# Two transformer layers on one core: a table of priority offsets for the list scheduler, and accumulators zeroed by products

## The chip, the cores and the metric

The kernel runs on one core of a Trainium2 chip. The core has five engines that run side by side, each with its own instruction stream: TensorE (PE, matrix products, with its weight loads shown apart as PEld), VectorE (DVE), ScalarE (ACT), GpSimd (POOL) and SyncE (SP, which here only issues DMA transfers). They wait for each other with semaphores. PE writes its products into PSUM, which has eight banks of 512 fp32 columns on 128 partitions; DVE and ACT read them from there. The metric is the time of one execution on the device, in microseconds (us); less is better.

## The reference

The input has 2048 tokens of width 512. Attention has 32 heads of width 16 and a causal window of 256 tokens; the feed-forward part has width 1792. The same weights are used twice.

```
x = A_x
x = x + _A_ref(_layernorm(x), A_wqkv, A_wo)          # sliding window attention
x = x + _B_ref(_layernorm(x), B_w1, B_b1, B_w2, B_b2)  # gelu(x @ w1 + b1) @ w2 + b2
x = x + _A_ref(_layernorm(x), A_wqkv, A_wo)
x = x + _B_ref(_layernorm(x), B_w1, B_b1, B_w2, B_b2)
return x
```

Inside `_A_ref`, scores are `q k^T / 4`, masked to `0 <= i - j < 256`, followed by a softmax, a product with `v`, and a product with `wo`.

## The kernel before

**Tiling.** X stays in SBUF as 16 tiles of 128 tokens (two layers make 32 tile visits). Attention works in blocks of 256 tokens: 8 in each layer, 16 in all. The feed-forward part works in ten jobs of two or four tiles.

**One attention block.** `lnq` and `kv` normalise the two tiles (statistics on DVE in `L547` and `L549`, the inverse root on POOL in `L551` and `L554`, the normalised tile xn on DVE in `L557`), transpose them on PE, and form Q, K and V. K is written with every second head masked to zero (`L625`). `visit` forms the scores: ten visits for each block, 64 small products each, into four banks; ACT takes the exponential from PSUM into E (`L699`). `mask` multiplies E by the causal mask on DVE (`L711`) or POOL (`L714`). `pv` multiplies E with V, to which a column of ones is appended, so that the sum of each softmax row comes out as one more row. Its result is copied from PSUM into OD on DVE (`L766`) or ACT (`L768`).

**Normalising.** For each half block, seven DMAs on SP do it: Dc gathers the sums from OD (`L769`), DVE takes the reciprocal (`L772`), scr_r writes it to DRAM (`L774`), Rn reads it back spread over the partitions (`L776`), and four copies move the odd heads inside OD (`L779`). Then OT = OD x Rn on DVE or POOL (`L784`), and `outproj` multiplies OT with Wo on PE. The residual is added on DVE (`L590`), the tile is normalised again, and POOL adds the second bias (`L819`).

**Feed-forward.** `mlp` multiplies with W1; the gelu runs on ACT directly from PSUM (`L858`), or after a copy with bias by DVE (`L846`) from SBUF (`L849`). Then it multiplies with W2 and adds the residual; in the last layer each finished tile is stored (`L870`).

**Order.** All this is given to a planner, `_Plan`, as nodes: engine, planned duration in ns, what is read and written, a priority `prio` (smaller goes first), an allocation of PSUM banks, and for some nodes alternatives `alt` on another engine with a handicap. `_Plan.run` is a list scheduler: it walks through planned time, and for each free engine it takes the ready node with the smallest priority. A handicap is added to the priority for the alternative engine (`ACT_H = 300` for copies on ACT, `POOL_H = 60` for masks on POOL), so it also decides which engine takes the node. What comes out is one fixed order for each engine, the engine of each movable node and the banks; `_Sched` then puts in the semaphore waits. On the chip each engine follows its order whatever the real durations are. Priorities run by block: block b starts at `200.0 * b`; inside it, a visit g stands at `16 * g`, the two halves of `pv` stand 80 apart, and the projections of the next block stand at 110 (Q) and 140 (K, V).

**Start.** Two DVE memsets (`L503`) set all eight PSUM banks to zero, and everything on PE waits for them. SP issues the loads in the order of their priorities: X tiles 0 to 1, 2 to 3, the three parts of Wqkv (`L516`), X 4 to 7, Wo, X 8 to 15, W1 (`L523`), W2 (`L524`), b2b (`L527`), b1raw (`L526`). In the profile all products that a helper issues have the line `L32`, and all transposes `L36`.

## Time and profile before

| | us |
|---|---|
| median of 3 runs (551.79 to 552.99) | 552.06 |
| the profiled execution | 548.19 |
| its span, first to last instruction | 546.5 |
| mean granted clock of PE | 0.956 of full speed |

The costliest groups of instructions, with the number of them, their busy time and the mean of one:

| engine, what | count | busy us | mean ns |
|---|---|---|---|
| ACT exponential, E from PSUM (`L699`) | 330 | 305.8 | 1009 |
| POOL masks (`L714`) | 96 | 112.5 | 1182 |
| DVE masks (`L711`) | 160 | 75.2 | 493 |
| ACT gelu from PSUM (`L858`) | 92 | 51.1 | 584 |
| ACT copies of OD (`L768`) | 21 | 21.5 | 1022 |
| DVE copies of OD (`L766`) | 11 | 13.4 | 1218 |
| DVE zeroing of PSUM (`L503`) | 2 | 3.5 | 1765 |

Busy times of different engines overlap, and a busy PE is modelled from the size of its products. "Granted clock" is the share of PE's full clock that the chip let through. The chain of waits follows the work back from the last instruction to what released each step; an engine's time that is not on it was hidden behind other work. Times in a list of the timeline are counted from the start of the span.

### The profile page before, as it was taken

The numbers are of one execution on the slowest core, as the hardware profiler recorded it, in microseconds if no ns is written. First come the engines' busy times: TensorE is split into PE (matmuls) and PEld (weight loads), VectorE is DVE, ScalarE is ACT, GpSimd is POOL, SyncE is SP. The second block draws the span as 40 slices with busy tenths as digits, with TensorE's granted clock in tenths as the row PEclk, the third lists the DMA queues.
The fourth block names the chain that finished last, engine by engine and source line by source line (L and its number), as shares of the span: only waits on it lengthen the run. The fifth ranks groups of instructions, "written<-read, shape, count | busy, mean of one in ns | idle before, by whom it ended". The sixth has DMA issues, their size and how long they took to land.

```text
span 546.5 us, 19716 instructions
## 1 busy us (share of the span) xinstructions
PE 458.2 (84%) x8849; PEld 246.2 (45%) x8945; DVE 358.9 (66%) x684; ACT 437.7 (80%) x521; POOL 222.5 (41%) x306
## 2 busy tenths in 40 slices
PE   3878697889579998899978879997898788969997
PEld 2545255455344443445444444443444343434644
DVE  6889675578586766886596768864576565764241
ACT  2798678788887898899899889898769987797633
POOL 6576523544264232652275225571144431422030
PEclk9979799999799999999999999997999989979999
DMA  8801101011111101110111101100121101111110
GB/s 276 312 13 52 38 12 36 22 35 31 35 33 34 35 4 39 32 37 25 34 34 34 33 10 39 52 14 22 34 61 45 33 3 48 59 34 38 35 49 20
DMA packets 26401, 25.01 MB, mean 46 GB/s; under 512 B 11596, under 2 KB 19660, under 8 KB 26316
## 3 DMA queue, kind: packets, MB, share of 16 engines
q1 hardware_dynamic: 26316, 23.74, 14.6%
q8 instruction: 70, 1.15, 0.9%
q14 instruction: 15, 0.12, 0.1%
HBM read 16.39 MB, written 2.62 MB: 35 GB/s over the span
## 4 chain that ended last, share of the span: by engine, by line
PE 44%; DVE 19%; DMA 18%; ACT 8%; SPq 5%; issue 4%; POOL 0%; DVEq 0%
PE ps L32 43%; DMA Rn<-scr_r 12%; ACT E L699 5%; SPq L779 4%; DMA scr_r<-Rc 4%; DVE OT L784 3%; DVE KT L625 3%; DVE E L711 3%; DVE stat L547 2%; DMA Dc<-OD 2%; DVE X L590 2%; ACT OD L768 2%; PE ps L36 1%; DVE QT L534 1%; DVE gT L846 1%
## 5 line engine op out<-in xcount | busy, mean ns | idle before, releaser
L699 ACT ACTIVATE E<-ps 128x1024 bf16<-128x1024 f32 (+1 forms) x330 | 305.8, 1009 | 26.5 <-PE ps L32 24.4
L714 POOL TENSOR_TENSOR E<-E,mask 128x512 bf16<-128x512 bf16 x96 | 112.5, 1182 | 153.5 <-ACT E L699 153.4
L32 PE MATMUL ps<-xnTB,W_sb 128*128 128x512 bf16 (+1 forms) x531 | 107.8, 340 | 6.3 <-issue 1.9
L32 PE MATMUL ps<-W_sb,gT 128*128 128x512 bf16 x407 | 102.1, 380 | 5.1 <-issue 2.1
L711 DVE TENSOR_TENSOR E<-E,mask 128x512 bf16<-128x512 bf16 x160 | 75.2, 493 | 35.4 <-ACT E L699 35.0
L32 PE MATMUL ps<-QT,KT 32*64 32x320 bf16 (+4 forms) x3072 | 71.2, 268 | 18.2 <-ACT E L699 14.2
L32 PE MATMUL ps<-xnTA,Wqkv_sb 128*128 128x256 bf16 x512 | 72.6, 284 | 8.2 <-DVE KT L625 4.6
L590 DVE TENSOR_TENSOR X<-X,ps 128x512 bf16<-128x512 bf16 x64 | 43.5, 683 | 48.0 <-PE ps L32 47.8
L32 PEld LDWEIGHTS ps<-xnTB,W_sb 128*128 128x128 bf16 x560 | 50.5, 99 | 48.3 <-issue 6.8
L858 ACT ACTIVATE gT<-ps,b1T 128x512 bf16<-128x512 f32 (+1 forms) x92 | 51.1, 584 | 17.5 <-PE ps L32 17.2
L32 PEld LDWEIGHTS ps<-W_sb,gT 128*128 128x128 bf16 x448 | 40.0, 98 | 49.0 <-issue 5.4
L32 PE MATMUL ps<-E,Va 64*17 64x128 bf16 (+3 forms) x3840 | 52.1, 240 | 11.5 <-DVE E L711 3.2
L32 PEld LDWEIGHTS ps<-QT,KT 32*64 32x64 bf16 x3072 | 28.7, 105 | 70.3 <-ACT E L699 48.2
L32 PEld LDWEIGHTS ps<-xnTA,Wqkv_sb 128*128 128x128 bf16 x512 | 46.1, 101 | 27.8 <-DVE KT L625 6.1
L551 POOL TENSOR_SCALAR veps<-statmv 128x1 f32<-128x1 f32 x64 | 16.0, 258 | 93.7 <-DVE statmv L549 93.2
L32 PEld LDWEIGHTS ps<-E,Va 64*17 64x17 bf16 x3840 | 41.0, 88 | 27.4 <-PE ps L32 8.4
L768 ACT ACTIVATE OD<-ps 128x1024 f32<-128x1024 f32 x21 | 21.5, 1022 | 28.8 <-PE ps L32 28.6
L846 DVE TENSOR_SCALAR gT<-ps,b1T 128x512 bf16<-128x512 f32 (+1 forms) x48 | 32.6, 681 | 17.3 <-PE ps L32 16.4
L547 DVE BATCH_NORM_STATS2 stat<-X 128x6 f32<-128x512 bf16 x64 | 43.1, 683 | 0.9
L784 DVE TENSOR_TENSOR OT<-OD,Rn 128x256 bf16<-128x256 f32 x46 | 23.7, 546 | 30.2 <-DMA Rn<-scr_r 29.9
L36 PE MATMUL ps<-ident,xn 128*128 128x128 bf16 x256 | 25.7, 232 | 21.0 <-DVE xn L557 9.9
L625 DVE TENSOR_TENSOR KT<-ps,parmask 128x1024 bf16<-128x1024 f32 x32 | 38.8, 1217 | 6.6 <-PE ps L32 6.5
(44 smaller groups left out, 394.7 us busy)
## 6 DMA issues: line engine op xcount, KB each, us to landing
Rn<-scr_r SPq DMA_DIRECT2D x32, 256.0 KB
OD<-OD SPq DMA_DIRECT2D x128, 32.0 KB
W_sb<-in_B_w_dram SPq DMA_DIRECT2D x2, 1792.0 KB
out_dram<-X SPq DMA_DIRECT2D x16, 128.0 KB
Wqkv_sb<-in_A_wqkv_dram SPq DMA_DIRECT2D x3, 512.0 KB
X<-in_A_x_dram SPq DMA_DIRECT2D x1, 1024.0 KB
X<-in_A_x_dram SPq DMA_DIRECT2D x2, 256.0 KB
X<-in_A_x_dram SPq DMA_DIRECT2D x1, 512.0 KB
```

The costliest lines, as they stand in the source:

```text
L32: return self.e.matmul(*a, **k)
L36: return self.e.transpose(*a, **k)
L547: add("dve", lambda e, B: e.bn_stats(stat6[:, k6, :], X[:, t, :]), 590, reads=["X%d" % t], writes=["st%d" % k6], prio=prio)
L590: add("dve", lambda e, B: e.tensor_tensor(out=X[:, t, :], in0=X[:, t, :], in1=ps[:, B[g][0], :], op=ALU.add), d_psum(512), reads=["X%d" % ...
L625: add("dve", lambda e, B, g=g, i=i: e.tensor_tensor(out=KT[:, kb, :, 2 * i : 2 * i + 2, :].rearrange("p a c q -> p a (c q)"), in0=ps[:, B[ ...
L699: a = (add("act", lambda e, B, g_=g_, gi=gi, o=o, e1=e1, n=n: e.activation(E[:, 2 * gi : 2 * gi + 2, e1 : e1 + n], ps[:, B[g_][0] : B[g_][ ...
L711: add("dve", lambda e, B: e.tensor_tensor(out=Ew, in0=Ew, in1=Mw, op=ALU.mult), 340.0, lock=True, reads=["E%d%s" % (es, x) for es in ess f ...
L714: alt=(("pool", lambda e, B: e.tensor_tensor(out=Ew, in0=Ew, in1=Mw, op=ALU.mult), POOL_M * n, POOL_H),))
L768: alt=(("act", lambda e, B: e.activation(OD[:, s, :, :], ob(B), AF.Copy, scale=1.0), d_act(1024), ACT_H),))
L784: mul = lambda e, B, c=c, o=o: e.tensor_tensor(out=OT[:, bs, c, :], in0=OD[:, s, 0, o : o + 256], in1=Rn[:, rs, o : o + 256], op=ALU.mult)
L846: add("dve", lambda e, B, g=g, fc=fc: e.tensor_scalar(out=gT[:, fc, 0:M], in0=ps[:, B[g][0], 0:M], scalar1=b1T[:, fc : fc + 1], scalar2=No ...
L858: gelu_last[0] = add("act", lambda e, B, g=g, fc=fc: e.activation(gT[:, fc, 0:M], ps[:, B[g][0], 0:M], AF.Gelu_apprx_tanh, bias=b1T[:, fc ...
```

## The change

`_Plan` gets two strings, `tune`. Every different triple of engine, rounded priority and duration gets a number in the order in which it first occurs; the character at that number in the first string, minus 80 (the letter P is zero), is added to the node's priority, and the one in the second string, times four, is added to the handicaps of its alternatives. The characters span -46 to +46. The first string has 1597 characters, 1382 of them not P; the second has 1576, 339 of them not P.

The two DVE memsets of PSUM become one memset of a new SBUF tile `zero` (128x512) and eight products of it with itself, one for each bank; that node is added twice (`NZ = 2`).

The planned duration of the Dc transfer goes from 1900 to 1980 ns, that of Rn from 3000 to 3600 ns.

```diff
-    def __init__(self, pools):
+    def __init__(self, pools, tune=("", "")):
+        self.keys = {}
+        self.tune = tune
...
         i = len(self.nodes)
+        k = self.keys.setdefault((eng, round(prio, 3), dur), len(self.keys))
+        step, lean = (float(ord(t[k]) - 80) if k < len(t) else 0.0 for t in self.tune)
+        prio += step
+        alt = tuple((e2, f2, d2, h2 + 4.0 * lean) for e2, f2, d2, h2 in alt)
...
-            alts=((eng, fn, dur, 0.0),) + tuple(alt), done=False,
+            alts=((eng, fn, dur, 0.0),) + alt, key=k, done=False,
...
+    NZ = 2
...
+        zero = sb("zero", [P, D])
...
+        TUNE = ((
+            '&J"Od*TQ)4I5KHPatpSx_#@QBTlr]Q~2IE5b"~STUK]UAS{6p[cVbHmkZEPYPeB"p)Zp_PP~_~"\\KPDEM0K[]QQB~LGP%K)7PNqP'
...
+        ), (
+            'PPPPPPPPPPPPPPPPPPPPPPPPPPPPQPMPPPPPPPPPP"PUPPPPPP*PPPPPPPPrPPiiPP~PPXAPP>7PPPP~PPPPP,PPJ8PP]PP)PPPC'
...
-        })
+        }, TUNE)
...
-        for h in range(2):
-            add("dve", lambda e, B, h=h: e.memset(ps[:, 4 * h : 4 * h + 4, :], 0.0), 1680, writes=["ps:init%d" % h], prio=-200)
+        add("dve", lambda e, B: e.memset(zero[:], 0.0), 120, writes=["zero"], prio=-300)
+
+        def clear(e, B):
+            for b in range(8):
+                r = e.matmul(ps[:, b, :], zero[:, 0:P], zero[:], start=True, stop=True)
+            return r
+
+        for h in range(NZ):
+            add("pe", clear, 8 * mm(512), reads=["zero"], writes=["ps:init0", "ps:init1"], prio=-200, geo="f")
...
-                    ["Dc%d" % rs], reads=ods, prio=pr - 50, dur=1900.0, issue=660.0)
+                    ["Dc%d" % rs], reads=ods, prio=pr - 50, dur=1980.0, issue=660.0)
...
-                    ["Rn%d" % rs], reads=["SR%d" % rs], prio=pr - 50, dur=3000.0, issue=710.0)
+                    ["Rn%d" % rs], reads=["SR%d" % rs], prio=pr - 50, dur=3600.0, issue=710.0)
```

In the first string the ninth character onward belongs to the loads: `)4I5KHPatpSx`, for X 0 to 1, X 2 to 3, the queries, keys and values of Wqkv, X 4 to 7, Wo, X 8 to 15, W1, W2, b1raw and b2b.

More of the change, by code (lines that the diff above doesn't have):

```diff
@@ L462, in bass_interleave_layers__sliding_block__dense_activation_gelu__prompt_kernel @@
         psb = ps[:].bitcast(dt.bfloat16)
+        TUNE = ((
+            '&J"Od*TQ)4I5KHPatpSx_#@QBTlr]Q~2IE5b"~STUK]UAS{6p[cVbHmkZEPYPeB"p)Zp_PP~_~"\\KPDEM0K[]QQB~LGP%K)7PNqP'
+            'SYa8ZVg9&-o"xVPP?bdDD;l/^ACPp]QPU;M+hSXU<ST+GPrs-PP\\\\@0^PP;xPh=SLXi;"VHP`nM9/zBpHIKbWauVL@"?NMW\\Ps=Q'
+            'mTUCC~"YX?GoopNO[eUw`MeO^ERPPDobLTF"PFYj"IULPL.P",&qW"J3qr"t~PUKP[O\'U}PECP~,[PJ.\'K.UQePBZQv\\:pXl"?j~'
+            'X{.abZ^tSbFQ~~5Xf\\@%PP^\\pPPS)8`b`.IP]Ncq3a7JtPlEv-]PQP$QPK&PPT`PPOkHPAWYV]@TL^S"Pmb*P6,*viVOPPJA"RuP'
+            '(ZEukBLP"J|qPdP"P.PROQNDO-:~2f&FGkB2P"fPd(P\'kN@DU<HPJBB-PPN}~=F"PrPNHY:G"I~R1lPesI6TRR6%J1VWPP]3Oh4G'
+            'PG<~],g@}Q3j"PGTdR[\\Lj"RDF8e^oPH]SR"N.VIixPAP\\MPI.|PPB"PT^H`O"S<Pa&OP{P|$ecPT&jP-pPMTSDuuPSP\\@PUzPx_'
+            'AATa\'iLH7w@6W~RY~o&PSbXL#~NPy%X|z~APyPPL`#UgABNJbNm?TOPh"9d[>O&K4WYiPJpPG_aM:0kSRdy7PgevHP^P\'?o,~60O'
+            '@:PZQTQtP"`PX8jhPlLE^<wPI=LYIPBX}GRPUyEPP.=hZe-^l8kSJT~PP0F\\S)EP-1RPvNRh*gV~>O~fPireN8_OBXMK3P@4WSjY'
+            'E7"K8PC~HMT(+QPBPSPJE"P-,@\'KE2M~Th-XE=VXPQl\\YP^P8XPPPnLY+OPI*P]#PT]LXfQcX"Z%\\\\Z\\8=^g?^PX6XRMIWPPT=s}'
+            'PcZ>P9y9encgw~XweXg4yJP~HJ~JK`ZSPm@@:_NE,,YO;M?PR]PR@KjxASi,~#"~K}+(PP_Q4jXTPKSP"PXP"_|"PgP8T$+-TF]j'
+            'pwH*]LUFOQaLP~LP"k>,GM((P~PP.~2\'TW$IPV+HPX>FR@LaPSz\\][`~~[TmKfO*PqI%4{P3SCT[|Y~G5rHc`H~Wa\\N`F&a^>n\\P'
+            "ePP)_qBYIGFxpP6~Y0jNanSNVPPET/J@@PGPP[RXI#a6W?M=Yp<c8:4{'VKR?PYBAt@~:wmJ@fYf%@KdPW|~]P~PYP`PIM~=YY??"
+            'ckTD"K"m~EPPWa)h"bW>U(~EJU~2$aQ<~>IM2XN?T8Pr)a/~AKP`P@~PWPx~PXPPJ^[H2OP~9U~-Q~bMLF|u___ysvYLDDqinXq~'
+            'hiT@F+rWSMNH"JpP"+ZQ)BN]u%ryPQxn"TOPPb"PO7inbQ.P"+SPgIPO(YeV.HXQEMWK(0>XURy41P:^H]&M;r:_u?~PU*\\PaPNS'
+            'IEMU\\~P+5kDP&0Ce:VZM"Pdi7DSkYPP,;qPiSf?V""gGJT/O~vAPH|$YP""+lIJYFT8T_JVt~a"+Z"NLd8\\AaXW*ZP:xz~"OOOFC'
+            '\'LPjuiOJMN&P;u@O/PEPPcC2{J_kCm[VP~"n,:^SSP",OP}[/DPMVqODp&@~?Ic]N"QXM>HXPC~w?IPPPq"9<PW`GuGMB&P-Q'
+        ), (
+            'PPPPPPPPPPPPPPPPPPPPPPPPPPPPQPMPPPPPPPPPP"PUPPPPPP*PPPPPPPPrPPiiPP~PPXAPP>7PPPP~PPPPP,PPJ8PP]PP)PPPC'
+            'mPmPPPPP,PPPPPPPP(PPPPPPPPPKPPPPPPPSPaPPPsPPePPnRPPPPPMCPP"}PP~PsPPPPPGPPCPPP3PPFLPP#~PPPPPPP"PPPPPP'
+            'PPrPPPPPPPPP?PPPPPPP9PsPPPPPP?PP>PPPhPPT8PPq"PPPP"PPPPPTPPZ|PPPPPPPPPPPPPPPPPPPPPPP~PP~rPP-TPDPPPPPO'
+            'PPPPPPPP"PPPPPPPPPBPPPPPPPhPVPPPlPPVPPi~PP[PPT"PPfJPPGPWPPPPP@PP@SPPPPPPPPPPPPPPPPPPPPPPP1PP6CPPxBPZ'
+            'PPPPPePPPPPPPP~PPPPPPPPPzPPPPPPPIPOPPPPPPPPP=KPPMPPP,PP8XPP[PPPPPPP~PP"~PPNPP_:PPn~P=PPPPP"PPPPPPPP6'
+            'PPPPPPPPPnPPPPPPP\'PPPPP~PPAPPj"PPPPP~^PPSaPP_PHPPPPPPPPZ[PPPPPPPPPPPPPPPPPPPPPPPPPPPPPP0,PPyQPEPPPPP'
+            '"PPPPPPPP"PPPPPPPPPePPPPPPPSP1PPP2PP~PP:PPPmPPBUPPzOPP_PkPPPPP-PP~\\PP"PPP"PP)mPwPPPPPPPPPPPPPPFPPPPP'
+            'PPPP~PPPPPPP"PDPPP@PPPPP"XPP_PPU8PPulPP]PlPPPPPPPPP~PPPPPPPPPPPPPPPPPPPPPPPPPPPZPP_DPP[PPPPPPPP~PPPP'
+            'PPPPgPPPPPPPPPPPPPPPPP[PLPPPFPPPPPM4PP"PP2%PPPWPP`PPPPPPP?PP+GPPpPP~-PPGPP~PPPPPUPPPPPPPP6PPPPPPPPP"'
+            'PPPPPPPPP\\PPPPPP"PP@^PPPPP"+PPNmPPbPPPPPPPmPPSIPPPPPPPPPPPPPPPPPPPPPPPPPPPEPPPVPPS_PLPPPPP=PPPPPPPPT'
+            'PPPPPPPPPKPPPPPPPPPHPPPRPP]PPPPPPPPP;IPP""PP<PxPPPPPMPP1bPPPPPT"PP*|PPPPPPP)PPPPPPPPPPPPPPPPPP6PPPPP'
+            'PP"PLPPPZPPMPPP"PP"PP+wPP4]PPvPQPPPPP"PPfyPPPPPPPPPPPPPPPPPPPPPPPPPPPP6PPS"PPFBPPPPPPP8PPPPPPPPWPPPP'
+            'PPPPPkPPPPPPPoPfPPPSPPPPPNPPP?PP-4PPX"PPPP~PPPPPjPPP/PP(PP:0PP(ZP=PPPPPNPPPPPPPP(PPPPPPPPPDPPPPPPPjP'
+            'WPPPPPPPPPPAPP:PP~uPP~MPPPPzPPPPP3PP"aPPPPPPPPPPPPPPPPPPPPPPPPPPPPNPPNLPPLXPPPPPPPPPPPPPPPPfPPPPPPPP'
+            'P5PPPP7PPaPP?xPPNPPkaPP[PPPfPAPPPPPuPP3"PPwPPS?PPP#P3PPPPPOPPPPPPPP"PPPPPPPPP"PPPKPPE6PP>PPK`PPnPPPa'
+            'PRPPPPPPPPqBPPPPPPPPPPPPPPPPPPPPPPPPPPPPPPP|qPPN]PTPPPPPTPPPPPPPPiPPPPPPPPPu'
+        ))
```

## The prediction

> **What bounds the kernel now.** I read the busy shares first, then the granted clock in stretches, then the chain of waits, then what each engine waited for. The profiled execution is 548.19 us: a span of 546.5 us and 1.69 us around it. The median of the runs, 552.06 us, is 0.71% above it; sums are made in the span and carried over with +1.69 and x1.0071.

> ```profile
> PE 458.2 (84%) x8849; PEld 246.2 (45%) x8945; DVE 358.9 (66%) x684; ACT 437.7 (80%) x521; POOL 222.5 (41%) x306
> PEclk9979799999799999999999999997999989979999
> PE 44%; DVE 19%; DMA 18%; ACT 8%; SPq 5%; issue 4%; POOL 0%; DVEq 0%
> ```

> No engine is full. PE and ACT are both some 80% busy and hand work to each other (scores to exponentials to value products), and less than half of the chain is PE. So the order decides, not the amount of work. The clock row shows a few slices below full speed; stretches cut around them:

> ```profile
> 27.00:40.00 13.00, 9.44 (x229) 5.48 (x214) 11.18 (x29) 12.11 (x14) 10.17 (x16) 0.74 0.05 10
> 54.00:75.00 21.00, 15.57 (x370) 8.34 (x355) 13.23 (x28) 12.81 (x16) 9.98 (x12) 0.76 0.11 32
> 137.00:170.00 33.00, 23.14 (x627) 12.89 (x617) 21.61 (x42) 26.39 (x32) 13.07 (x16) 0.84 0.11 30
> 170.00:366.00 196.00, 174.33 (x3472) 89.94 (x3518) 145.19 (x275) 175.10 (x197) 90.40 (x113) 1.00 0.11 31
> 366.00:380.00 14.00, 9.95 (x114) 4.39 (x121) 4.79 (x11) 12.37 (x16) 2.55 (x2) 0.76 0.10 29
> 434.00:446.00 12.00, 7.89 (x116) 4.17 (x116) 4.29 (x9) 10.73 (x13) 2.54 (x2) 0.86 0.10 29
> 482.00:498.00 16.00, 12.47 (x203) 6.17 (x206) 9.08 (x16) 11.56 (x14) 6.26 (x8) 0.68 0.15 40
> ```

> Columns: stretch, length, then busy time of PE, weight loads, DVE, ACT and POOL, then the granted clock, then DMA. One long stretch, 170 to 366, runs at full clock with PE and ACT both 89% busy (174.33/196 and 175.10/196). Six short ones, 109 us together, have PE 78.46 us busy at a length-weighted clock of 0.78: (13x0.26 + 21x0.24 + 33x0.16 + 14x0.24 + 12x0.14 + 16x0.32)/109 = 0.22 is missing. At full clock that is 61.3 us of products; at the 89% of the long stretch it would take 68.9 us. **The six cost 109 - 68.9 = 40 us, 6.7 us each.** Before the low clock comes a group of PE gaps:

> ```profile
> 56.59 0.19 PE L32 MATMUL ps<-E,Va 64*17 64x64 bf16 x1 [1.59 <-POOL OT L784]
> 63.17 0.42 PE L32 MATMUL ps<-QT,KT 32*64 32x192 bf16 x16 [1.99 <-ACT E L699]
> 161.32 0.40 PE L36 MATMUL ps<-ident,xn 128*128 128x128 bf16 x4 [1.57 <-DVE xn L557]
> 372.70 1.03 PE L36 MATMUL ps<-ident,xn 128*128 128x128 bf16 x8 [2.82 <-ACT E L699]
> 488.41 3.19 PE L32 MATMUL ps<-Wo_sb,OT 128*128 128x512 bf16 x7 [1.32 <-DVE OT L784]
> ```

> In brackets: idle time and its releaser. Each is PE standing at an instruction whose input or bank isn't ready. All of them are places in a fixed order, which is what the table moves. The last row shows the price of the low clock too: 7 products of 512 columns in 3.19 us, a start every 0.43 us.

> **Part 1, the zeroing.** The chain of waits begins with it:

> ```profile
> 1.29 1.76 DVE ps L503
> 3.43 1.76 DVE ps L503
> 5.20 1.13 DVE stat L547 x2
> ```

> Two DVE memsets, 1.77 us each, go; a 128x512 memset of SBUF (planned 0.12 us) and 16 products of 512 columns come. The statistics start when DVE is free and the first X has landed. The DMA's bytes by half microseconds reach 256 KB between 3.0 and 3.5 us and 512 KB at 4.0, while the statistics ran at 5.11; so DVE gains between 0 and 1.7 us, and I take 1.0. The zero products lie in 1.6 to 8.3 us, in which PE does nothing. At the 0.43 us of the row above all 16 take 6.9 us and end at 8.5; at the warm rate of 0.22 (16 such products in 3.63 us at 506.71) they take 3.5. Transposes would be ready at 7.3, so at worst PE is 0.2 us later than now. In exchange, it is warm: the first 16 projection products took 3.31 us (9.86) and the next 16 took 1.91 (14.08), which is worth 1.4 us at most, if the weights have landed. I take 1.0 of it. **Start: -2.0 us (bounds +0.2 and -3.1).** Without the idle PE as a cover it would cost 3.5 to 6.9 us.

> [...]

> **Part 2, the loads.** SP issues in order. With the first entries of the table the keys of Wqkv go ahead of the queries (-125 and -106), X4 to 7 ahead of the values (-104 and -102), W2 ahead of W1 (-60 and -57), and b2b last. W1 may land 5 us later (1792 KB at 350 GB/s), but all loads were in by 26 us and the first product with W_sb starts at 68.2 us. b2b's issue holds SP for 7.55 us (12.58 to 20.13), and the bias b1raw behind it now goes ahead of it. Cost 0; with that cover gone, 5 us.

> **Part 3, longer planned transfers.** On the chain the Rn transfer is 18 long pieces of 3.42 to 4.45 us, about 3.7 in the mean; the plan had 3.0 and now has 3.6. Dc takes 1.98 and is now planned at 1.98. So the output projections move later, by some 0.68 us, behind other PE work. PE waited for OT directly:

> ```profile
> PE ps L32 <- DVE OT L784: 6.6, 4, 1.8
> PE ps L32 <- POOL OT L784: 2.5, 2, 1.6
> PE ps L32 <- ACT E L699: 16.1, 21, 2.0
> ```

> Six waits, 9.1 us, 1.5 us each: 0.68 x 6 = 4.1 us go, bounds 0 and 9.1. Two of the six gap groups, at 56 and 488 us, begin with such a wait, so this is not added to what follows.

> **Part 4, the table.** 1382 of 1597 offsets of the first table are not zero, up to 46 either way, where a block of 256 tokens is 200 wide and its two halves stand 80 apart. Nothing is added to any engine. All instructions and all 224 normalising DMAs on SP (7 for each of 32 half blocks) are placed anew; SP has no work to lose, but one Rn behind a Dc that waits for its OD could be held by as much as the longest such wait, 17.7 us. The second table moves copies between ACT and DVE: 32 of OD (1.02 us on ACT, 1.22 on DVE), and masks between POOL (1.18) and DVE (0.49). ACT's movable copies are 43 us in all (21.5 + 8.4 + 4.7 + 4.2 + 4.2); the leans have both signs (mean +7.5 x 4 = 30 against a threshold of 300 for OD), so I take 0, bounds -43 and +43 of ACT's time, none of which reaches the span one to one.
> What the order can win is bounded by the long stretch: all six gone is -40 us. It could lose as well: each new group of gaps is 6.7. I take three of six, -20: two begin with the OT wait of part 3, and the one at 366 is a transpose placed before the exponential that frees its bank, 2.82 us in one wait. The start at 27 is different: only exponentials of the first block can run then. The stretches at 137 and 434, with exponentials waited for again and again, I leave.

> **Sum.** 546.5 - 2.0 - 20 = 524.5 us of span; (524.5 + 1.69) x 1.0071 = **530 us**, its own range 519 to 541 (one and a half stretches either way).

> **Rivals.** (A) The order reaches the long stretch's density throughout: 546.5 - 2 - 40 = 504.5, which is 510 us. For it: both engines already hold 89% for 196 us. Against it: PE still waits 16 us for exponentials, and a fuller PE makes ACT the bound. Chance 0.14.
> (B) The plan's durations do not fit the chip closely enough, so gaps move without getting fewer: only the start and at most the direct OT waits are won, 546.5 - 2 - (0 to 4.1), 546 to 550 us. For it: the plan knows no clock, and the low clock stretches every product after a gap. Chance 0.19.
> (C) Slower: the order opens two more groups of PE gaps, each followed by the low clock. The place is the head of a block, where the projections of the next block, whose offsets are among the largest (q 22, v 26 in the mean), are moved ahead of or behind the exponentials that PE needs covered. 546.5 - 2 + 13.4 = 557.9, which is 563 to 564 us. It decides as soon as there is one stretch more than now, since 6.7 exceeds the start's 2.0. For it: PE and ACT both wait for each other now, and one wait of 1.6 us is enough. Against it: six such places already exist, so a new order has more to mend than to break. Chance 0.17.

> **How the numbers follow.** Forecast 0.50, A 0.14, B 0.19, C 0.17. About 0.2%, 1.1 us, is what a measurement of this kernel can tell from no change. Faster: 0.50 + 0.14 + 0.14 of B = 0.78; same: 0.03 of B; slower: 0.17 + 0.02 of B = 0.19. The range of 510 to 556 leaves out half of A and most of C, some 0.19.

> **What would show it.** Start: first statistics before 4.5 us, 16 products before 8.5 us, and the 16 projection products in under 2.5 us. Order: three or fewer stretches below a clock of 0.9, a mean clock above 0.97, PE's waits for OT under 5 us. Busy sums of ACT and DVE within 10 us of now. Wrong would be a mean clock at or under 0.956, or PE's waits for exponentials above 16 us.

## The result, and the profile after

| | before | changed |
|---|---|---|
| median of 4 runs, us | 552.40 (551.79 to 552.99) | 512.71 (510.15 to 515.33) |
| ratio, with its 95% interval | | 0.928 (0.923 to 0.934) |
| profiled execution, us | 548.19 | 515.33 |
| its span, us | 546.5 | 513.6 |
| mean granted clock of PE | 0.956 | 0.977 |

The kernel became 7.2% faster, nearly 40 us; the two profiled spans lie 32.9 us apart. Two executions among the experiments below took 1091.81 and 2416.8 us; the ratios leave them out, and the profile of the run without the second string is of the first. The page of the changed kernel, in the order in which it was read before: busy time, granted clock in 40 slices, chain by engine.

```profile
PE 454.8 (89%) x8862; PEld 243.4 (47%) x8961; DVE 355.9 (69%) x695; ACT 434.8 (85%) x515; POOL 215.0 (42%) x302
PEclk9998699999979999999999999999999999899999
PE 56%; DVE 19%; ACT 9%; DMA 6%; issue 4%; POOL 3%; SPq 1%; DVEq 0%; POOLq 0%
```

The busy time of PE, ACT and DVE is what it was, within 3.5 us, and POOL has 7.5 us less; it is the span around it that shrank. For PE that hides two things: 5.55 us of zero products are new, and all its other products together took 458.2 - (454.8 - 5.55) = 9.0 us less, which goes with the higher granted clock. On the chain the DMAs fell from 18% to 6% and PE rose from 44% to 56%. PE's idle time in the span went from 546.5 - 458.2 = 88.3 us to 513.6 - 454.8 = 58.8 us. (Both traces lack about 1% of the product records, 96 and 99, so the difference holds better than either number.) PE's waits for exponentials, for OT and at the start, before (those that the prediction doesn't show) and in the changed kernel (total us, times, longest):

```profile
PE ps L36 <- DVE xn L557: 9.9, 2, 8.3
PE ps L36 <- ACT E L699: 6.8, 3, 2.8
```

```profile
PE ps L32 <- ACT E L749: 7.3, 17, 1.2
PE ps L36 <- ACT E L749: 1.2, 1, 1.2
PE ps L32 <- DVE OT L834: 1.5, 1, 1.5
PE ps L32 <- POOL OT L834: 0.2, 1, 0.2
PE ps L32 <- DVE zero L545: 1.2, 1, 1.2
```

Waits for exponentials were 16.1 us at the products and 6.8 at the transposes, 22.9 together, and are 8.5. Waits for OT were 9.1 and are 1.7. The first wait of the kernel was 8.3 us (for the first normalised tile) and is 1.2 us; zero products fill the rest. These three make up 14.4 + 7.4 + 7.1 = 28.9 of the 29.5 us that PE's idle time fell. The zero products only fill time at the start in which PE stood idle before; without their 5.55 us the idle time fell by 24 us. So of the 32.9 us of span some 24 are idle time of PE and 9 are shorter products. Stretches of the changed kernel (length, busy time of PE, weight loads, DVE, ACT, POOL, granted clock, DMA):

```profile
42.00:66.50 24.50, 17.52 (x487) 9.41 (x488) 16.91 (x33) 20.51 (x24) 9.61 (x12) 0.72 0.20 55
147.00:157.50 10.50, 7.79 (x225) 4.59 (x228) 8.43 (x16) 8.03 (x12) 5.14 (x6) 0.67 0.14 40
157.50:444.50 287.00, 261.72 (x5206) 134.52 (x5269) 206.93 (x397) 258.31 (x292) 119.36 (x148) 1.00 0.13 35
444.50:451.50 7.00, 6.31 (x179) 3.23 (x182) 4.50 (x10) 4.79 (x6) 0.00 (x0) 0.76 0.15 50
```

Three low-clock stretches are left of six, 42 us of 109. The long stretch at full clock is 287 us in place of 196, and denser too: PE 91% busy (261.72/287) where it was 89%. Missing records lower both: two kernels below whose traces have them all show 92% with the old order (179.90 of 196 us, the zeroing alone) and 95% with the new one (272.68 of 287 us, the zeroing taken back). The start, as the timeline has it:

```profile
0.91 0.27 DVE L545 MEMSET zero<- 128x256 uint32 x1 [0.91 <-PEq L973]
1.24 5.55 PE L32 MATMUL ps<-zero 128*128 128x512 bf16 x16 [1.24 <-DVE zero L545]
3.74 1.29 DVE L597 BATCH_NORM_STATS2 stat<-X 128x6 f32<-128x512 bf16 x2 [2.56 <-DMA X<-in_A_x_dram]
8.99 3.65 PE L32 MATMUL ps<-xnTA,Wqkv_sb 128*128 128x256 bf16 x32 [1.12 <-DVE xn L607]
```

The zero products end at 6.8 us, the statistics wait for X and no longer for memsets, and the first 32 projection products take 0.11 us each; in the kernel before, the first 16 took 0.21.

### The profile page after: what moved, and what is told of

Same layout as the page of the kernel before. It is cut to its first block, busy times and chain, and to the rows that moved or that the text cites. A ratio compares the mean times of both kernels' runs of the same rounds, so it can differ in the third digit from the quotient of the medians.

```text
span 513.6 us, 19757 instructions
## 1 busy us (share of the span) xinstructions
PE 454.8 (89%) x8862; PEld 243.4 (47%) x8961; DVE 355.9 (69%) x695; ACT 434.8 (85%) x515; POOL 215.0 (42%) x302
## 4 chain that ended last, share of the span: by engine, by line
PE 56%; DVE 19%; ACT 9%; DMA 6%; issue 4%; POOL 3%; SPq 1%; DVEq 0%; POOLq 0%
PE ps L32 55%; ACT E L749 7%; DMA Rn<-scr_r 5%; DVE KT L675 3%; DVE stat L597 3%; DVE X L640 3%; DVE E L761 2%; DVE xn L607 2%; DVE OT L834 2%; PE ps L36 2%; DMA scr_r<-Rc 2%; SPq L829 1%; DVE QT L584 1%; ACT OD L818 1%; POOL rstd L604 1%
## 5 line engine op out<-in xcount | busy, mean ns | idle before, releaser
L764 POOL TENSOR_TENSOR E<-E,mask 128x512 bf16<-128x512 bf16 x88 | 103.8, 1192 | 113.6 <-ACT E L749 113.4
L32 PE MATMUL ps<-xnTB,W_sb 128*128 128x512 bf16 (+1 forms) x533 | 107.9, 337 | 5.8 <-issue 2.1
L32 PE MATMUL ps<-W_sb,gT 128*128 128x512 bf16 x401 | 103.5, 380 | 4.1 <-issue 2.7
L761 DVE TENSOR_TENSOR E<-E,mask 128x512 bf16<-128x512 bf16 x168 | 77.6, 488 | 31.7 <-ACT E L749 30.8
L32 PE MATMUL ps<-QT,KT 32*64 32x320 bf16 (+4 forms) x3072 | 70.4, 266 | 13.0 <-ACT E L749 6.2
L32 PE MATMUL ps<-xnTA,Wqkv_sb 128*128 128x256 bf16 x512 | 69.8, 278 | 5.0 <-DVE xnTB L584 1.9
L32 PEld LDWEIGHTS ps<-xnTB,W_sb 128*128 128x128 bf16 x560 | 50.0, 98 | 47.4 <-issue 4.4
L32 PEld LDWEIGHTS ps<-W_sb,gT 128*128 128x128 bf16 x448 | 39.3, 98 | 46.2 <-issue 8.3
L32 PE MATMUL ps<-E,Va 64*17 64x128 bf16 (+3 forms) x3840 | 51.5, 237 | 10.5 <-DVE E L761 4.1
L32 PEld LDWEIGHTS ps<-QT,KT 32*64 32x64 bf16 x3072 | 28.4, 105 | 63.4 <-ACT E L749 41.8
L908 ACT ACTIVATE gT<-ps,b1T 128x512 bf16<-128x512 f32 (+1 forms) x92 | 50.0, 585 | 9.4 <-PE ps L32 9.3
L32 PEld LDWEIGHTS ps<-xnTA,Wqkv_sb 128*128 128x128 bf16 x512 | 45.6, 99 | 24.3 <-issue 3.4
L32 PEld LDWEIGHTS ps<-E,Va 64*17 64x17 bf16 x3840 | 40.5, 87 | 27.7 <-issue 9.8
L869 POOL TENSOR_TENSOR X<-X,b2b 128x512 bf16<-128x512 bf16 x32 | 38.3, 1197 | 12.2 <-DVE xn L607 11.9
L818 ACT ACTIVATE OD<-ps 128x1024 f32<-128x1024 f32 x22 | 22.6, 1026 | 21.2 <-PE ps L32 21.2
L834 POOL TENSOR_TENSOR OT<-OD,Rn 128x256 bf16<-128x256 f32 x22 | 17.5, 800 | 53.1 <-DMA Rn<-scr_r 49.5
```

The source lines that it names most:

```text
L32: return self.e.matmul(*a, **k)
L761: add("dve", lambda e, B: e.tensor_tensor(out=Ew, in0=Ew, in1=Mw, op=ALU.mult), 340.0, lock=True, reads=["E%d%s" % (es, x) for es in ess f ...
L764: alt=(("pool", lambda e, B: e.tensor_tensor(out=Ew, in0=Ew, in1=Mw, op=ALU.mult), POOL_M * n, POOL_H),))
L818: alt=(("act", lambda e, B: e.activation(OD[:, s, :, :], ob(B), AF.Copy, scale=1.0), d_act(1024), ACT_H),))
L834: mul = lambda e, B, c=c, o=o: e.tensor_tensor(out=OT[:, bs, c, :], in0=OD[:, s, 0, o : o + 256], in1=Rn[:, rs, o : o + 256], op=ALU.mult)
L869: add("pool", lambda e, B: e.tensor_tensor(out=X[:, t, :], in0=X[:, t, :], in1=b2b[:], op=ALU.add), 1110, reads=["X%d" % t, "b2b"], writes ...
```

## The experiments

The change has three parts that can be taken apart: the zero products, the two planned durations, and the table with its two strings. The theory was that the order does the work and that the start is worth about 2 us. All runs below are compared with the kernel before on their own chip; its median there lay between 547 and 552 us, so ratios carry further than medians.

**The zeroing alone**, put into the kernel before:

```diff
-            add("dve", lambda e, B, h=h: e.memset(ps[:, 4 * h : 4 * h + 4, :], 0.0), 1680, writes=["ps:init%d" % h], prio=-200)
+            add("pe", clear, 8 * mm(512), reads=["zero"], writes=["ps:init0", "ps:init1"], prio=-200, geo="f")
```

> The kernel before with the zero products (twice eight) in place of the two DVE memsets, no table, planned transfers as before. Theory (the zeroing is worth its place in the start alone, about 2 us, and the order does the rest): 549 to 551 us, a mean clock of 0.95 to 0.96, and low-clock stretches at the places of before. Rival (the warm start is what keeps the clock up later): under 540 us and fewer low stretches.

Measured: 546.4 us, ratio 0.998 (0.994 to 1.002). By the ratio it can't be told from the kernel before; the median lies under the expected range, and 3.7 us under that of the kernel before on this chip (550.08). The clock is 0.956 as before. The first exponential starts at 17.00 us in place of 19.75, yet the first value product comes at 33.36 in place of 32.11. The timeline of this run shows where 2.75 us went; first SP's issues, then PE:

```profile
12.36 9.11 SPq L536 DMA_DIRECT2D b2b<-in_B_b_dram  x1
21.52 0.92 SPq L535 DMA_DIRECT2D b1raw<-in_B_b_dram  x1
28.22 0.32 PE L32 MATMUL ps<-QT,KT 32*64 32x320 bf16 x1 [3.78 <-DMA b1raw<-in_B_b_dram]
28.47 0.18 PE L36 MATMUL ps<-ident,b1raw 14*128 14x14 bf16 x1
```

SP takes 9.11 us to issue the broadcast load of b2b, b1raw stands behind it, and PE, now early, waits 3.78 us for a bias that it needs much later. In the changed kernel the table puts b1raw ahead of b2b, and its transpose runs at 24.74 us without a wait.

**The zeroing taken back**, everything else as changed (the numbering of the table held in step):

```diff
-        add("dve", lambda e, B: e.memset(zero[:], 0.0), 120, writes=["zero"], prio=-300)
...
-            add("pe", clear, 8 * mm(512), reads=["zero"], writes=["ps:init0", "ps:init1"], prio=-200, geo="f")
+        PL.keys["held"] = len(PL.keys)
+        for h in range(2):
+            add("dve", lambda e, B, h=h: e.memset(ps[:, 4 * h : 4 * h + 4, :], 0.0), 1680, writes=["ps:init%d" % h], prio=-200)
```

> The changed kernel with the two DVE memsets back and no zero products; the numbering of the table is kept in step. Theory: 2 to 3 us above the changed kernel, 514 to 516 us, because only the start moves. Rival (the warm start carries more): over 522 us.

Measured: 513.38 us, ratio 0.936 (0.931 to 0.942). And **half of the zero products**:

```diff
-    NZ = 2
+    NZ = 1
```

> The changed kernel with eight zero products in place of sixteen. Theory: the first projections run at half rate for a while, some 1 to 1.5 us later at the start, and nothing of it is left at the end, as the run with the memsets left nothing: 511 to 516 us. Rival (PE's state at the start decides where the low clock falls later): over 518 us and other stretches.

Measured: 514.05 us, ratio 0.935 (0.931 to 0.940). By medians the zeroing is worth 0.7 us and the second set of eight 1.3 us; by ratios up to 4.5 us, with intervals that overlap. The first lies a little under its expected range, the second within it. That agrees with the expected 2 us and can't be told from nothing; it is at most a small part of the 40.

**The durations without the table:**

```diff
-        }, TUNE)
+        })
```

> The changed kernel with both strings of the table empty: zero products and the longer planned Dc and Rn remain. Theory (the offsets carry the gain): 543 to 550 us, PE's direct waits for OT falling from 9 us to about 5. Rival (the planner only lacked the right transfer times, the table adds little): under 530 us.

Measured: 534.91 us, ratio 0.977 (0.972 to 0.983), between the two expectations. Against the zeroing alone the two numbers in the plan are worth 11.5 us. What DVE and PE waited for in this run:

```profile
DVE OT L834 <- DMA Rn<-scr_r: 18.8, 12, 7.2
PE ps L32 <- POOL OT L834: 1.0, 3, 0.4
PE ps L32 <- DVE OT L834: 0.7, 1, 0.7
```

PE's direct waits for OT are 1.7 us, as low as with the table, where they were 9.1 before and 7.6 with the zeroing alone; the waits for exponentials did not fall (17.8 us at the products, 12.3 with the zeroing alone). DVE's wait for Rn was 33.3 us with the zeroing alone. **Which duration it is** was tried with Dc back at 1900:

```diff
-                    ["Dc%d" % rs], reads=ods, prio=pr - 50, dur=1980.0, issue=660.0)
+                    ["Dc%d" % rs], reads=ods, prio=pr - 50, dur=1900.0, issue=660.0)
```

> The changed kernel without the table and with Dc planned at 1900 again; Rn stays at 3600. With both durations it was 534.9 us, with neither 546.4. Theory (Rn is the transfer that was planned too short, by 0.7 us, and Dc's 80 ns matter little): 531 to 539 us. Rival (Dc is what moves the order): 543 to 550 us.

Measured: 537.73 us, ratio 0.979 (0.973 to 0.985). Rn alone brings 8.7 of the 11.5 us by medians, and 10.5 of 11.3 by ratios; Dc alone was not tried.

**The table on the old durations** (the numbering kept as it is with the new ones):

```diff
         prio += step
+        if dma:
+            dur = {1980.0: 1900.0, 3600.0: 3000.0}.get(dur, dur)
```

> The changed kernel with the planned Dc and Rn back at 1900 and 3000 ns, same table, same numbering. Theory A (each offset is good by itself, the longer transfers only spare the waits for OT): 4 to 9 us above the changed kernel, 517 to 522 us. Theory B (the table fits one exact plan, and a change of two durations turns it into just another order): 535 to 560 us.

Measured: 556.06 us, ratio 1.013 (1.008 to 1.019). That is theory B of the expectation. The four corners, in us, with the ratios:

| | no table | table |
|---|---|---|
| Dc 1900, Rn 3000 | 546.4 (0.998) | 556.1 (1.013) |
| Dc 1980, Rn 3600 | 534.9 (0.977) | 512.7 (0.928) |

On the new durations the table wins 22.2 us; on the old ones the same table loses 9.7. The changed kernel was timed apart from the other three, beside a kernel before of 552.4 us where theirs took 550.1; by ratios the table wins 27 us and loses 8.5. With the old durations the waits for the transfers are back:

```profile
DVE OT L836 <- DMA Rn<-scr_r: 33.1, 18, 7.2
PE ps L32 <- DVE OT L836: 6.5, 4, 3.1
PE ps L32 <- ACT E L751: 16.5, 20, 2.4
```

DVE waits for Rn as long as with the zeroing alone, and single waits of PE for OT reach 3.1 us, where the longest was 1.8 before.

**A random table** of the same kind, quarter size, on the new durations:

```diff
-        step, lean = (float(ord(t[k]) - 80) if k < len(t) else 0.0 for t in self.tune)
+        step, lean = (0.25 * float(ord(t[k]) - 80) if k < len(t) else 0.0 for t in self.tune)
...
-        }, TUNE)
+        }, tuple("".join(np.random.RandomState(7).permutation(list(t))) for t in TUNE))
```

> The changed kernel with both strings put into a random order (numpy, seed 7) and a quarter of their size, so that the plan still closes. Theory (what counts is which offset stands where; a random one is just another order, and with the right transfer times it does no better than no table): 535 to 565 us. Rival (any loosening of the regular order spreads the load): under 528 us.

Measured: 559.93 us, ratio 1.021 (1.013 to 1.028), 25 us slower than no table. Half of that is the start, because the random offsets put both loads of W ahead of the last part of Wqkv:

```profile
3.40 5.07 SPq L573 DMA_DIRECT2D W_sb<-in_B_w_dram  x1
11.40 1.38 SPq L566 DMA_DIRECT2D Wqkv_sb<-in_A_wqkv_dram  x1
23.60 3.81 PE L32 MATMUL ps<-xnTA,Wqkv_sb 128*128 128x256 bf16 x17 [8.00 <-DMA Wqkv_sb<-in_A_wqkv_dram]
```

The first exponential starts at 29.60 us, where it starts at 16.98 without a table. So offsets of this kind don't help wherever they stand, but this is one random table, and how much it loses behind the loads was not measured by itself. The same table at a quarter of its size in its own order was not run either.

**The second string empty:**

```diff
-        }, TUNE)
+        }, (TUNE[0], ""))
```

> The changed kernel with the second string empty: no offsets on the handicaps that decide which engine takes a movable copy or mask. Theory (the priorities carry the gain, the leans have both signs and nearly cancel): within 3 us of the changed kernel, 510 to 517 us, ACT busy within 5 us of 434.8. Rival (the leans balance ACT against DVE and POOL, and that is a good part of the gain): over 522 us.

Measured: 512.22 us, ratio 0.931 (0.925 to 0.936). No gain of the leans can be seen. The sign for ACT's busy time stays open, since no profile of this run can be compared.

**The first 800 entries only:**

```diff
-        }, TUNE)
+        }, tuple(t[:800] for t in TUNE))
```

> The changed kernel with the first 800 entries of both strings and zeros behind them, so that about the first half of the program has its offsets. Theory (the gain is local and adds up stretch by stretch): about half of the 22 us that the table is worth, 521 to 529 us, with the first half as in the changed kernel. Rival (a partly filled table breaks the plan, as the other durations did): over 535 us.

Measured: 523.05 us, ratio 0.954 (0.947 to 0.960). That is 11.9 of the 22.2 us (by ratios 13 of 27). The 165th of the 330 exponentials ends at 238.4 us, at 241.2 in the changed kernel and at 252.3 without a table. Cut in time, the table keeps its worth: the gain is made stretch by stretch.

**What a gap costs.** The prediction put 6.7 us on each group of gaps, low clock included. Eight extra waits were put into the part that ran at full clock: a DMA of 3.5 KB starts when PE's last work is done, and PE's next group waits for it.

```diff
+        stalls = [165e3 + 33e3 * x for x in range(8)]
         for i in order:
...
+                if stalls and nd["start"] >= stalls[0]:
+                    stalls.pop(0)
+                    S_.op("sp", lambda e: e.dma_start(b1raw[:], B_b1.rearrange("(c p) -> c p", p=P)),
+                          reads=["mark"], writes=["b1raw"], dma=True, start=nd["start"], end=nd["start"])
...
+                  writes=phys(nd["writes"]) + (["mark"] if nd["eng"] == "pe" else []), dma=nd["dma"],
```

> The changed kernel with eight extra waits of PE, spread over the part that ran at full clock (157 to 444 us): at each, PE waits for a small DMA that starts when its last work is done, some 2 us. It measures what one gap costs. Theory as predicted (a gap is followed by the low clock, 6.7 us each): 545 to 567 us and up to eight new low stretches. Rival 1 (a gap costs its own length, no more): 525 to 531 us, clock as before. Rival 2 (slack takes it up): under 520 us.

Measured: 528.51 us, ratio 0.962 (0.955 to 0.968), clock 0.981 to 0.990.

```profile
PE ps L32 <- DMA b1raw<-in_B_b_dram: 13.1, 8, 1.9
```

Each wait idles PE for 13.1 / 8 = 1.6 us and costs (528.5 - 512.7) / 8 = 2.0 us by medians, 2.3 by ratios. No slack takes it up. Behind the five waits before 325 us the clock stays at 1.00; the profile's mean of 0.990 leaves room for one low stretch later, by an estimate (0.010 x 523.3 = 5.2 us of clock lost, 3.4 of it before 325 us), and the changed kernel has one of its own there, at 444.5 us. That is rival 1 of the expectation, with a price a little above the gap's own length. Then **two at each place**, with one group of products between:

```diff
-        stalls = [165e3 + 33e3 * x for x in range(8)]
+        stalls = [165e3 + 33e3 * x for x in range(8) for y in range(2)]
```

> As the kernel with eight extra waits, but two in a row at each place, with one group of products between them, so that PE is busy for well under half of some 4 us there. The single waits cost 15 us in all, 1.9 us each, with no new low clock. Theory (what brings the low clock is a stretch of about 3.5 us in which PE is less than half busy, not one gap): the pairs cost more than twice the singles, 550 to 570 us, with up to eight new low stretches in the part from 157 to 444 us. Rival (gaps cost their own length however they lie): 513 + 16 x 1.9 = 543 us, 538 to 547, clock as before.

Measured: 552.83 us, ratio 1.010 (1.005 to 1.015), clock 0.957. PE's wait, then the stretches around the first two places:

```profile
PE ps L32 <- DMA b1raw<-in_B_b_dram: 26.2, 16, 2.7
```

```profile
171.00:174.50 3.50, 1.81 (x8) 0.55 (x6) 0.15 (x1) 1.71 (x3) 0.72 (x1) 1.00 0.18 59
174.50:178.00 3.50, 2.07 (x11) 1.20 (x12) 1.09 (x4) 1.50 (x2) 0.00 (x0) 0.64 0.01 1
178.00:181.50 3.50, 3.50 (x37) 1.39 (x36) 1.07 (x3) 2.80 (x4) 0.00 (x0) 0.87 0.00 0
210.00:213.50 3.50, 1.48 (x20) 0.81 (x10) 1.53 (x5) 2.77 (x4) 3.18 (x5) 0.93 0.02 7
213.50:217.00 3.50, 2.11 (x51) 1.40 (x58) 1.02 (x2) 0.00 (x0) 0.28 (x1) 0.50 0.01 1
217.00:220.50 3.50, 3.50 (x120) 2.19 (x105) 2.59 (x7) 1.75 (x3) 0.00 (x0) 0.59 0.02 5
```

The low clock now follows at each of the four places before 325 us, with 3.5 us at 0.57, 0.50, 0.73 and 0.64. Of the 0.043 x 552.3 = 23.7 us of clock lost in the whole run an estimated 12.0 lie before 325 us, so about as much comes later; at which of the other four places is not shown. A pair costs 5.0 us by medians and 5.6 by ratios, of which two single waits are 4.0 to 4.6: if the low clock is what is left, it adds an estimated 1 us to each place, and the gaps are the rest.

**A version with fewer thin stretches.** The first string was searched anew, with the condition told in the expectation.

```diff
+        NEW = {0: -37, 1: -15, 3: -3, 4: 38, 5: -14, 6: 28, 7: 34, 8: -46,
...
-        }, TUNE)
+        }, ("".join(chr(80 + NEW[k]) if k in NEW else c for k, c in enumerate(TUNE[0])), TUNE[1]))
```

> The changed kernel with another first string, found by changing offsets at random and keeping those with which the plan is as long as the changed kernel's but has fewer stretches of 3.5 us in which PE is planned under half busy. Theory (such stretches bring the low clock and cost about 1.7 us each beyond their gaps): 504 to 511 us, mean clock above 0.985, two low stretches or fewer. Rival (the plan's stretches are not where the chip's are, and an order found for one plan is only as good as another): 512 to 520 us, clock as in the changed kernel.

Measured: 509.10 us (507.10 to 509.82), ratio 0.928 (0.923 to 0.933), clock 0.987 to 0.996. The clock is higher, and the median lies 3.6 us under the changed kernel's; but the ratios are the same, and the profile still has three low places (42, 52 and 196 us). The expected two low places or fewer did not come, and the expectation's price of 1.7 us for each was not measured; the pairs gave about 1. Whether it beats the changed kernel stays open.

## Why the prediction was right, and where its sizes were off

The forecast was 530 us with a range of 510 to 556, and 512.7 lies at its fast end, nearest to rival A (510). That range spans the rivals too; the forecast's own range, 519 to 541 us, was missed, with 22 us forecast and 40 measured. Direction and mechanism hold: the engines have the same work but for the zero products, and PE's waits in a fixed order went. All the signs that were named came out: first statistics at 3.74 us, zero products done by 6.8, 16 projection products in under 2 us, three low stretches, a clock of 0.977, waits for OT of 1.7 us, ACT and DVE busy within 3 us of before.

**Part 1, the start (-2.0).** Right for the start, where with the zeroing alone the first exponential came 2.75 us earlier. At the end of the kernel the three runs on it give 0.7 to 4.5 us, none of it clear of nothing.

**Part 2, the loads (0).** Put at 0, and a small term was left out. With the earlier start PE waits 3.78 us for b1raw when it stands behind b2b (3.1 us in the run without the table), and the table's new order is what spares that. The 42 us of cover for W1 were there: no wait for it was seen.

**Part 3, the planned transfers (-4.1, not added).** Mis-sized. The two numbers are worth 11.5 us without the table. The direct waits for OT fell by 7.4 us, from 9.1 to 1.7, within the bounds of 0 to 9.1 but well above the 4.1. What was left out is that a duration moves the whole order, for every instruction behind a wrong due time is placed by it; of the 11.5 us against the zeroing alone no more than 7.6 - 1.7 = 5.9 shows as a wait of PE for OT. That the rest comes from the other instructions was not taken apart and is not shown.

**Part 4, the table (-20).** 22.2 us measured on the new durations (27 by ratios), so the size is nearly right, but by luck, not by the count it was made from. The count was six stretches at 6.7 us, three of which go. Three did go, but a pair of extra gaps cost 5.0 to 5.6 us, and only an estimated 1 us of it was the low clock. Granted clock lost fell from 23.9 us (the six stretches) to 24.5 x 0.28 + 10.5 x 0.33 + 7 x 0.24 = 12.0 us; at the pairs' 1 us for each of three stretches that would be an estimated 3 us of the 40. The stretches are longer than those behind a pair, though, and PE's products took 9.0 us less, so the low clock's part is estimated at 3 to 9 us and is not shown more closely. The larger part of the gain is the gaps themselves, and some of it lies where the clock was never low: the long stretch became denser, 89% to 91%. The forecast let nothing change there.

**The sum.** Parts 3 and 4 were taken as one gain of 20 us where they are 11.5 + 22.2. Adding the forecast 4.1 would have given (546.5 - 2.0 - 20 - 4.1 + 1.69) x 1.0071 = 526 us; with the measured 11.5 and 22.2 it is 516 us.

**Rivals.** A expected all six stretches gone and 89% throughout; three are left and the long stretch is above 89%, so its time is nearly right by another way. B, that the plan fits the chip too badly for its order to win, is false for the new durations and true for the old ones: there the table costs 9.7 us. C, an order that opens more gaps, is what the table on the old durations shows, at 556 us; the prediction gave 563 to 564. The random table, at 560 us, owes half of its loss to the loads. C's argument that one wait of 1.6 us is enough for the low clock does not hold in general: behind five such waits the clock stayed at 1.00, and all eight left its mean at 0.981 to 0.990.

## What to carry to other kernels

When a planner sets a fixed order, first compare its durations with the trace: one transfer planned 0.7 us too short cost some 9 to 10 us here, more than twice what the waits that named it let expect. A table of offsets found for one plan need not suit another: the one that wins 22 us here was worse than none when two durations went back, so search again after a correction. Where PE is as full as here, price its gaps at their own length or a little more (2.0 to 2.3 us for a wait of 1.6), and look for places where several lie close together (5.0 to 5.6 us for two).

## What the runs showed of the hardware

In these runs the low clock followed stretches in which PE worked little; a single wait of 1.6 us did not bring it by itself. Eight single waits of 1.6 us left the mean clock at 0.981 to 0.990; pairs within some 4 us left it at 0.957 in the profiled run, with 3.5 us at 0.50 to 0.73 behind each of the four places before 325 us. The same place in two kernels shows how little made the difference; first the changed kernel, then the one with the memsets:

```profile
266.00:269.50 3.50, 1.75 (x80) 0.98 (x85) 3.50 (x4) 1.92 (x3) 3.26 (x6) 1.00 0.04 7
269.50:273.00 3.50, 3.25 (x52) 1.45 (x51) 3.17 (x7) 3.50 (x5) 0.51 (x1) 1.00 0.03 5
```

```profile
266.00:269.50 3.50, 1.53 (x43) 0.97 (x42) 3.50 (x5) 1.95 (x3) 3.50 (x6) 1.00 0.01 2
269.50:273.00 3.50, 3.50 (x57) 1.40 (x55) 1.99 (x5) 3.04 (x4) 0.27 (x1) 0.52 0.03 6
```

```profile
42.73:46.14 3.41, 3.14 (x49) 1.52 (x50) 2.05 (x4) 2.65 (x4) 0.90 (x2) 0.50 0.16 34
46.14:52.97 6.83, 4.24 (x160) 2.71 (x166) 5.80 (x11) 6.83 (x8) 2.03 (x3) 1.00 0.33 89
52.97:63.21 10.24, 7.95 (x151) 3.56 (x128) 5.97 (x11) 7.77 (x11) 4.37 (x4) 0.50 0.18 53
148.54:155.37 6.83, 5.23 (x178) 3.59 (x180) 5.23 (x10) 4.65 (x8) 3.60 (x4) 0.50 0.14 43
445.50:448.91 3.41, 3.08 (x108) 1.64 (x109) 1.98 (x5) 1.74 (x2) 0.00 (x0) 0.50 0.23 79
```

Cut in steps of that length, the place looks like this, first in the changed kernel, then with the eight extra waits:

```profile
264.60:268.00 3.40, 1.78 (x37) 1.24 (x36) 3.40 (x6) 2.88 (x4) 2.87 (x3) 1.00 0.01 2
268.00:271.40 3.40, 3.03 (x91) 1.63 (x92) 3.19 (x6) 2.34 (x4) 1.26 (x4) 1.00 0.03 5
```

```profile
266.80:270.20 3.40, 1.66 (x73) 0.99 (x71) 3.40 (x4) 1.82 (x3) 3.40 (x6) 1.00 0.03 7
270.30:273.50 3.20, 2.87 (x33) 1.07 (x23) 1.94 (x5) 3.10 (x4) 0.02 (x1) 0.50 0.03 5
```

At this place the clock stayed at 1.00 after PE was busy for 1.78 of 3.40 us and fell to 0.50 after 1.66. The edge was not as sharp everywhere: in the kernel before the clock stayed after 1.51 of 3.41 us (from 210.70 us) and fell after 1.86 (from 26.38), and in the changed kernel it fell after 2.00 (from 39.32).

At the start the sixteen zero products took 5.55 us, where all at the 0.43 us of the row at 488 us before would take 6.9 and all at 0.22 would take 3.5. In the trace ten of them started in the first 4.09 us, 0.41 us each, and the other six took 1.46, 0.24 each. So the short spacing came some 4.1 us after the first product.

A broadcast load's issue held SP for 7.55 us before and 9.11 us in the run with the zeroing alone, longer than any other issue in the start. The load alone is not the reason: in the changed kernel, where it comes last, it took 1.42 us, and the load of W1 ahead of it 5.03.

```profile
10.74 5.03 SPq L573 DMA_DIRECT2D W_sb<-in_B_w_dram  x1
15.81 1.42 SPq L577 DMA_DIRECT2D b2b<-in_B_b_dram  x1
```
